# A fused attention and gated-MLP kernel on one core: every second pair of the first chunk's score matmuls in other PSUM banks with VectorE copies, and v's loads three units earlier

## The chip, the cores and the metric

The kernel runs on one core of one Trainium2 chip. The metric is the device time of one execution in microseconds (us). The engines are named as the profile names them: PE (TensorE matmul), PEld (its weight load), DVE (VectorE), ACT (ScalarE), POOL (GpSimd), SP (SyncE), and SPq, POOLq, ACTq for what their queues issue or wait for.

## What is computed

Attention with a mixing of the heads before and after the softmax, and then a bilinear MLP on its output. Sizes: 4 batches, 12 heads, 448 positions, 64 values a head; 768 model columns, 1536 inner ones.

```
scores = scale * q @ k.T                      # per head
scores = einsum("bhij,hg->bgij", scores, w_pre)
attn   = exp(scores - max); attn /= sum + 1e-9
attn   = einsum("bhij,hg->bgij", attn, w_post)
x      = (attn @ v), heads side by side       # 1792 x 768
out    = ((x @ w_a) * (x @ w_b)) @ w_out
```

## The kernel before

**Tiles and order.** The 448 query rows of a batch are cut into chunks of 120, 120, 120 and 88 rows, so there are 16 chunks. For a chunk, `qk` (L219) is called six times. Call i multiplies the q of heads i and i + 6 (two row halves of TensorE) by their keys, into one tile `pst` of two PSUM banks (tag "t", one buffer), and ACT copies both banks at once into `s`, the chunk's scores in SBUF (L227). I call one such call a pair. `s` has two buffers, so chunk c writes where chunk c - 2 lay.

**Units.** A chunk's rows are then taken 20 at a time: a unit, 6 units in a chunk of 120 rows and 5 in the one of 88, 23 in a batch, 92 in all. `gather` (L232) brings a unit's rows of `s` into the order (row, head) on the partitions, with four transfers from SBUF to SBUF on SP's queue (`sb<-s`, L243); unit s + 3 is gathered in iteration s of the main loop (L575), into four buffers. In iteration s, `premix` (L252) multiplies unit s by w_pre into `mp`, `smax` (L265) takes the maximum on DVE and the exponential on ACT, `norm` (L276) works on DVE, and `postmix` (L289) of unit s - 1 multiplies by w_post into `pp`, which ACT copies into `pt` (L307). `av` (L309) multiplies a group of eight units by v into `xp`, two heads' pairs at a time, for the first group of a batch in units 9, 11 and 13, and a DVE copy takes `xp` out (L330).

**What sets the order around the change.** Everything is in program order on each engine, as written. The first chunk's six pairs come ahead of the main loop, one after the other (L558 to L566): its q parts are spread on DVE (`spread_q`, L205), its k parts are loaded on SP (L193), four ahead. Behind them come `setup_w` on DVE (L161), the gathers of units 0 to 3, and `warm_up(WARM3)`: 60 small matmuls into a tile of tag "x" whose result is not used (L136). The tags "m", "p" and "x" have two one-bank buffers each; "m" is next used by the premix, "p" by the postmix, and "x" by that warm-up and by `av`.

The pairs of later chunks are spread over the units. Those of the next batch's first chunk begin in unit 15 of a batch, two of them in that unit, and that chunk's first copy writes the buffer of `s` that the gather of unit 17 reads last. The last chunk of a batch begins in unit 9, and its first copy writes where unit 11 is gathered from.

**Loads.** POOL issues the loads of v, of q from the third chunk on, and of k from the second batch on. The main loop makes it wait once in each iteration for DVE's work of the unit before (`pace`, L118). The six parts of the next batch's v, 224 KB each, are loaded one in an iteration, from unit `V_AT` = 9 of a batch to unit 14 (L595 to L597), k's six parts in units 12 to 16, and q's parts in units 5, 8, 11 and 13 among others. `v` has two buffers for each half of the heads. The first batch's own v is loaded in units 2 and 4. The last batch loads nothing ahead.

After unit 91 the MLP runs from about 475 us to the end, nearly all of it back-to-back matmuls.

Of the kernel before, what the change touches and what calls it, by code (L numbers as in the profile page):

```python
# [7 lines left out]
F32 = mybir.dt.float32  # L8
# [13 lines left out]
def talking_heads_bilinear_kernel(  # L22
# [11 lines left out]
    nc = tc.nc  # L34
    B, _, G, S = k.shape
    H, D = 2 * G, 64
# [5 lines left out]
    QG = 3  # L42
# [18 lines left out]
    WARM3 = 60  # L61
    Q1E = 3
    KL = 3
    V_AT = 9
    LQ = 4
    scale = 1.0 / float(D) ** 0.5

# [1 line left out]
    for b in range(B):  # L69
        t0 = 0  # L70
        while t0 < S:
            n = min(CHUNK, S - t0)
# [23 lines left out]
    ps = ctx.enter_context(tc.tile_pool(name="ps", bufs=2, space=PSUM))  # L96
# [86 lines left out]
    kt, qraw, qt, vt = {}, {}, {}, {}  # L183
    st, sbt, mt, at, ant, ptt, pps, xps = {}, {}, {}, {}, {}, {}, {}, {}

    def load_v(b, i):

        g, e = divmod(i, 3)
        if e == 0:
            vt[b, g] = v_p.tile([P, H // 2, R, D], F32, tag=f"v{g}", name="v")  # L190
        nc.gpsimd.dma_start(out=vt[b, g][:, 2 * e:2 * e + 2], in_=v[b, g][:, 2 * e:2 * e + 2])
# [27 lines left out]
    def qk(c, i):  # L219
        b, t0, n = chunks[c]  # L220
        if c not in st:
            st[c] = big.tile([128, H, S], F32, tag="s", name="s")
        sp = ps.tile([128, 2, 512], F32, tag="t", name="pst", bufs=1)[:, :, :S]
        for g in range(2):
            rows = slice(D * g, D * g + D)
            nc.tensor.matmul(sp[:n, g], lhsT=qt[c, i // QG][rows, i % QG], rhs=kt[b, i][rows])  # L226
        nc.scalar.copy(st[c].rearrange("p (g i) s -> p i g s", g=2)[:n, i], sp[:n])  # L227
# [108 lines left out]
    for c in range(1, NC):  # L336
        b, t0, _ = chunks[c]
        a, e = max(starts[c - 1] - AH, 0), starts[c] - AH
        for i in range(G):
            at_s = qk_at[c, i] = i * Q1E // G if c == 1 else a + i * (e - a) // G  # L340
            items.setdefault(at_s, []).append((qk, c, i))
            if t0 == 0:
                after.setdefault(at_s - KL, []).append((load_k, b, i))
        ready[c] = qk_at[c, G - 1]
        for j in range(G // QG):
            if c > 1:
                when = max(qk_at[c, QG * j] - LQ, 0)
                after.setdefault(when, []).insert(0, (load_q, c, j))
            if c > 1 or j:
                after.setdefault(max(qk_at[c, QG * j] - 1, 0), []).append((spread_q, c, j))  # L350
    last_prep = ready[NC - 1]
    for a in range(NA - 1):
        b, u0, n = groups[a]
# [192 lines left out]
    with tc.manual_schedule():  # L546
# [11 lines left out]
        for i in range(G):  # L558
            if i == 1:
                spread_q(0, 1, nc.vector)  # L560
            if i + 4 < G:
                load_k(0, i + 4)
            if i == 2:
                load_q(1, 0)
                load_q(1, 1)
            qk(0, i)  # L566
# [8 lines left out]
        for s in range(NU + 2):  # L575
# [19 lines left out]
            b, i = divmod(s, NUB)  # L595
            if b + 1 < B and 0 <= i - V_AT < 6:
                load_v(b + 1, i - V_AT)  # L597
            for fn in todo_at.pop(s, ()):
# [89 lines left out]
        for j in range(B * KD):  # L688
            b, m = divmod(j, KD)
# [57 lines left out]
```

## Time and profile before

| what | us |
|---|---|
| median of 3 runs | 1013.9 |
| lowest and highest of the runs | 1010.79, 1014.28 |
| the profiled execution | 1010.31 |
| its span, first to last instruction | 1008.6 |
| PE busy in the span | 962.7 (95%) |
| ACT busy | 418.5 (41%) |
| DVE busy | 513.1 (51%) |
| POOL busy | 293.0 (29%) |

The mean granted TensorE clock over the span is 0.983 of full speed. Start times in the rows below are us from the span's start. In a timeline row stand the start, the duration from first to last instruction of the row, the engine, the line, the operation, its tiles, the count, and in brackets how long the engine had been idle before it and what ended that.

### The profile page before, as it was taken

Reading aid. Unit: us, or ns where it says so; the run is one execution under the profiler, and the core shown is the slowest. Engines: PE = TensorE matmul, PEld = TensorE weight load, DVE = VectorE, ACT = ScalarE, POOL = GpSimd, SP = SyncE. Lnnn points to the kernel's source line nnn. Section 1 sums busy time; section 2 is a strip of 40 time slices with the busy share of each in tenths; the row PEclk is TensorE's granted clock in tenths of the full one; section 3 lists DMA queues with packets and bytes.
Section 4 is the critical chain, followed back from the end, with each engine's and each line's share of the span. In section 5 each row is a group of like instructions: output and inputs, shape, how many; then the busy total and the mean of one; then the engine's idle time right before and its main releaser. Section 6 shows DMA issues by size and latency. Waiting matters only on the chain.

```text
span 1008.6 us, 17007 instructions
## 1 busy us (share of the span) xinstructions
PE 962.7 (95%) x6388; PEld 774.4 (77%) x6388; DVE 513.1 (51%) x1090; ACT 418.5 (41%) x854; POOL 293.0 (29%) x321
## 2 busy tenths in 40 slices
PE   7798899979999899988999999999999999999998
PEld 4465566646665566666889999999999998999997
DVE  1455355535555355567767565665555454432510
ACT  2675466756676566656321111111111133342521
POOL 2223011320123111112133323333233225555542
PEclk9999799989999899999999999999999999999999
DMA  3446233553346333348335333423333256556441
GB/s 117 156 137 199 95 123 123 156 164 97 123 136 191 104 131 119 114 155 260 112 105 188 134 118 138 146 97 139 114 139 136 85 215 244 192 202 257 146 137 68
DMA packets 63472, 146.60 MB, mean 145 GB/s; under 512 B 6252, under 2 KB 48000, under 8 KB 62368
## 3 DMA queue, kind: packets, MB, share of 16 engines
q1 hardware_dynamic: 58528, 131.11, 38.1%
q0 software_dynamic: 4864, 14.42, 5.1%
q8 instruction: 51, 0.84, 0.3%
q14 instruction: 29, 0.24, 0.1%
HBM read 80.23 MB, written 26.74 MB: 106 GB/s over the span
## 4 chain that ended last, share of the span: by engine, by line
PE 82%; DMA 11%; DVE 3%; ACT 2%; SPq 1%; issue 1%; POOL 0%; ACTq 0%; DVEq 0%
PE pp L296 13%; DMA sb<-s 10%; PE pst L226 7%; PE mp L263 7%; PE xp L321 6%; PE po L445 6%; PE po L446 6%; PE po L444 6%; PE pa L444 5%; PE pa L445 5%; PE pa L446 5%; PE pb L446 5%; PE pb L444 5%; PE pb L445 5%; ACT s L227 1%; DVE xhl L376 1%
## 5 line engine op out<-in xcount | busy, mean ns | idle before, releaser
L296 PEld LDWEIGHTS pp<-kr,a 124*112 124x112 f32 (+1 forms) x1440 | 159.7, 182 | 50.7 <-issue 33.0
L272 DVE TENSOR_REDUCE nm<-mp 124x1 f32<-124x448 f32 x180 | 104.2, 619 | 154.3 <-PE mp L263 154.3
L296 PE MATMUL pp<-kr,a 124*112 124x120 f32 (+1 forms) x1440 | 177.3, 278 | 2.8 <-ACT pt L307 1.7
L273 ACT ACTIVATE a<-mp,nm 124x448 f32<-124x448 f32 x180 | 112.7, 631 | 90.7 <-DVE nm L272 90.5
L226 PE MATMUL pst<-k,q 64*120 64x448 f32 (+1 forms) x384 | 100.1, 599 | 30.9 <-ACT s L227 30.8
L406 POOL TENSOR_TENSOR cvm<-cvm,cvr 128x768 int32<-128x768 int32 x36 | 67.0, 1860 | 211.6 <-DVE cvm L405 211.6
L434 POOL TENSOR_TENSOR wl<-rawo,wh 128x768 fp32r<-128x768 f32 x48 | 93.0, 1960 | 100.9 <-ACT wh L433 100.9
L307 ACT COPY pt<-pp 112x480 f32<-112x480 f32 x180 | 97.0, 574 | 51.7 <-PE pp L296 51.6
L456 ACT COPY sa<-pa 128x448 f32<-128x448 f32 x48 | 25.7, 536 | 221.7 <-PE pa L446 216.6
L121 POOL COPY tick<-rs 60x1 f32<-60x1 f32 x92 | 17.1, 186 | 344.9 <-DVE rs L280 344.9
L445 PE MATMUL pa<-xhl,wh 128*128 128x448 f32 x288 | 104.6, 363 | 1.9 <-DVE xhl L376 1.9
L445 PE MATMUL po<-hl,wh 128*128 128x448 f32 x288 | 104.5, 363 | 0.7 <-DVE hl L481 0.7
L444 PE MATMUL pa<-xhl,wh 128*128 128x448 f32 x288 | 104.6, 363 | 0.0
L446 PE MATMUL pa<-xhl,wl 128*128 128x448 f32 x288 | 104.4, 363 | 0.0
L444 PE MATMUL po<-hh,wh 128*128 128x448 f32 x288 | 104.4, 362 | 0.0
L446 PE MATMUL po<-hh,wl 128*128 128x448 f32 x288 | 104.4, 362 | 0.0
L446 PE MATMUL pb<-xhl,wl 128*128 128x448 f32 x282 | 102.3, 363 | 0.9 <-POOL wl L434 0.9
L226 PEld LDWEIGHTS pst<-k,q 64*120 64x120 f32 (+1 forms) x384 | 27.0, 175 | 98.5 <-ACT s L227 39.9
L444 PE MATMUL pb<-xhl,wh 128*128 128x448 f32 x282 | 102.2, 362 | 0.0
L445 PE MATMUL pb<-xhl,wh 128*128 128x448 f32 x282 | 102.2, 362 | 0.0
L227 ACT COPY s<-pst 120x896 f32<-120x896 f32 (+1 forms) x96 | 86.4, 900 | 36.6 <-PE pst L226 19.8
L263 PE MATMUL mp<-sb,wp 60*64 60x448 f32 x720 | 95.2, 564 | 3.8 <-ACT a L273 3.5
(64 smaller groups left out, 1373.1 us busy)
## 6 DMA issues: line engine op xcount, KB each, us to landing
sb<-s SPq DMA_DIRECT2D x356, 105.0 KB
raw<-in_w_ab_dram SPq DMA_DIRECT2D x24, 768.0 KB
rawo<-wod SPq DMA_DIRECT2D x24, 768.0 KB
hd<-hf SPq DMA_DIRECT2D x48, 224.0 KB
raw<-in_w_out_dram SPq DMA_DIRECT2D x12, 768.0 KB
v<-in_v_dram POOLq DMA_DIRECT2D x24, 224.0 KB, 6.0
xhl<-xd SPq DMA_DIRECT2D x12, 448.0 KB
hl<-hd SPq DMA_DIRECT2D x4, 1344.0 KB
```

Of the source, the lines that this page charges most:

```text
L226: nc.tensor.matmul(sp[:n, g], lhsT=qt[c, i // QG][rows, i % QG], rhs=kt[b, i][rows])
L227: nc.scalar.copy(st[c].rearrange("p (g i) s -> p i g s", g=2)[:n, i], sp[:n])
L263: nc.tensor.matmul(mt[u, i // 2][col:col + M], lhsT=wp[r:r + m, :M], rhs=tiles[i % 2][r:r + m])
L272: nc.vector.tensor_reduce(nm[:m], mp[:m], axis=AXX, op=ALU.max, negate=True)
L273: nc.scalar.activation(a[:m], mp[:m], ACTF.Exp, bias=nm[:m], scale=1.0, accum_out=rs[:m])
L296: nc.tensor.matmul(pp[:, r, :, :n], lhsT=an[:m, r * P:(r + 1) * P], rhs=kr[:m, :, :n])
L307: nc.scalar.copy(ptt[a][:P, :, :, o:o + n], pps.pop((u, j))[:, :, :, :n])
L406: lambda: nc.gpsimd.tensor_tensor(m, m, r, op=ALU.add),
L434: nc.gpsimd.tensor_tensor(ll[:, sl], raw, hh.bitcast(F32)[:, sl], op=ALU.subtract)
L444: nc.tensor.matmul(o, lhsT=hh[:, k0 + kk], rhs=mh[:, kk], start=(kk == 0), stop=False)
L445: nc.tensor.matmul(o, lhsT=hh[:, k0 + kk], rhs=ml[:, kk], start=False, stop=False)
L446: nc.tensor.matmul(o, lhsT=ll[:, k0 + kk], rhs=mh[:, kk], start=False, stop=(kk == n - 1))
```

## The change

`qk` treats the first chunk's pairs 1, 3 and 5 in another way. Each of the two heads gets a one-bank tile of its own, of tag "m" for pair 1, "p" for pair 3 and "x" for pair 5, and DVE copies each of the two out by itself. Pairs 0, 2 and 4 stay in `pst` with ACT's copy. Apart from that, `V_AT` goes from 9 to 6, so v's six parts for the next batch are issued in units 6 to 11 of batches 0, 1 and 2.

```diff
-    V_AT = 9
+    V_AT = 6
...
     def qk(c, i):
         b, t0, n = chunks[c]
         if c not in st:
             st[c] = big.tile([128, H, S], F32, tag="s", name="s")
+        if c == 0 and i % 2:
+            for g in range(2):
+                rows = slice(D * g, D * g + D)
+                sp = ps.tile([128, 512], F32, tag="mpx"[i // 2], name="psq")[:, :S]
+                nc.tensor.matmul(sp[:n], lhsT=qt[c, i // QG][rows, i % QG], rhs=kt[b, i][rows])
+                nc.vector.tensor_copy(st[c][:n, g * G + i], sp[:n])
+            return
         sp = ps.tile([128, 2, 512], F32, tag="t", name="pst", bufs=1)[:, :, :S]
```

## Rows read from the trace of the kernel before

**Rows 1.** The page's part 4: the chain of work that ended last, by engine and by line, in shares of the whole span.
```profile
PE 82%; DMA 11%; DVE 3%; ACT 2%; SPq 1%; issue 1%; POOL 0%; ACTq 0%; DVEq 0%
PE pp L296 13%; DMA sb<-s 10%; PE pst L226 7%; PE mp L263 7%; PE xp L321 6%; PE po L445 6%; PE po L446 6%; PE po L444 6%; PE pa L444 5%; PE pa L445 5%; PE pa L446 5%; PE pb L446 5%; PE pb L444 5%; PE pb L445 5%; ACT s L227 1%; DVE xhl L376 1%
```

**Rows 2.** The timeline of all engines from 0 to 45 us: the first chunk's pairs, the warm-up behind them, the first gather and the first premix.
```profile
5.51 1.03 PE L226 MATMUL pst<-k,q 64*120 64x448 f32 x4
...
6.10 0.79 DVE L211 COPY q<-qraw 128x360 f32<-128x360 f32 x1 [2.00 <-DMA qraw<-in_q_dram]
6.59 0.91 ACT L227 COPY s<-pst 120x896 f32<-120x896 f32 x1 [4.28 <-PE pst L226]
...
7.55 1.02 PE L226 MATMUL pst<-k,q 64*120 64x448 f32 x4 [1.01 <-ACT s L227]
...
9.68 0.81 POOL L211 COPY q<-qraw 128x360 f32<-128x360 f32 x1 [4.61 <-DMA qraw<-in_q_dram]
...
15.63 1.71 PE L226 MATMUL pst<-k,q 64*120 64x448 f32 x4 [1.00 <-ACT s L227]
...
17.28 4.44 PE L141 MATMUL warm<-ones 128*128 128x128 f16 x60
...
18.32 27.11 SPq L243 DMA_DIRECT2D sb<-s  x28
...
22.94 1.79 PE L263 MATMUL mp<-sb,wp 60*64 60x448 f32 x6 [0.33 <-DMA sb<-s]
```

**Rows 3.** The transfers' rate from 0 to 22 us, in 40 slices of 0.55 us each.
```profile
GB/s 0 0 0 92 264 348 295 257 211 344 282 244 287 376 393 379 81 16 0 0 0 134 196 5 0 0 0 0 0 0 0 0 0 0 30 0 121 124 127 127
```

**Rows 4.** All DVE copies of line 330, which take a PSUM bank out as the new copies do: durations in ns, least, median and most, and their shapes.
```profile
L330 DVE COPY xs<-xp x24: 557/656/658, 78.8 to 488.8; 128x480 f32<-128x480 f32 x16, 128x384 f32<-128x384 f32 x8
```

**Rows 5.** Stretches of the start: from and to, length, then busy us (and count) of PE, PEld, DVE, ACT and POOL, the granted clock, the DMA share and GB/s.
```profile
6.00:15.50 9.50, 4.61 (x20) 1.15 (x16) 1.77 (x6) 4.45 (x5) 2.19 (x3) 1.00 0.38 124
...
16.00:19.00 3.00, 3.00 (x21) 1.73 (x18) 0.00 (x0) 0.91 (x1) 0.00 (x0) 0.50 0.03 5
...
33.00:36.00 3.00, 3.00 (x15) 3.00 (x16) 0.00 (x0) 1.47 (x2) 1.27 (x2) 0.50 0.93 248
```

**Rows 6.** PE's timeline: the postmixes of units 0 and 1.
```profile
32.92 3.53 PE L296 MATMUL pp<-kr,a 124*112 124x120 f32 x16
...
41.26 1.89 PE L296 MATMUL pp<-kr,a 124*112 124x120 f32 x16
```

**Rows 7.** The chain that ended last, in order of time: start, us, what. These are its pieces on the gather's transfers in batch 0 (four of them) and in batch 1 (two).
```profile
47.94 8.21 DMA sb<-s
...
56.16 7.02 DMA sb<-s
...
63.20 8.59 DMA sb<-s
...
94.44 10.00 DMA sb<-s
...
195.30 10.05 DMA sb<-s
...
205.36 10.81 DMA sb<-s
```

**Rows 8.** Transfers issued between 56.16 and 63.20 us, other than the gather's: count, KB each, median us from issue to landing.
```profile
qraw<-in_q_dram POOLq DMA_DIRECT2D x1, 132.0 KB, 5.5
```

**Rows 9.** The same between 63.20 and 71.80 us.
```profile
v<-in_v_dram POOLq DMA_DIRECT2D x2, 224.0 KB, 6.0
```

**Rows 10.** The same between 195.30 and 205.34 us, with the gather's.
```profile
sb<-s SPq DMA_DIRECT2D x7, 105.0 KB
k<-in_k_dram POOLq DMA_DIRECT2D x3, 224.0 KB, 7.5
v<-in_v_dram POOLq DMA_DIRECT2D x2, 224.0 KB, 6.4
xd<-xs SPq DMA_DIRECT2D x1, 240.0 KB
qraw<-in_q_dram POOLq DMA_DIRECT2D x1, 180.0 KB, 6.6
```

**Rows 11.** ACT's timeline: the first copy of a batch's last chunk (unit 9 of batch 0 and of batch 1) and of the next batch's first chunk (unit 15 of batches 0, 1 and 2).
```profile
71.94 0.90 ACT L227 COPY s<-pst 88x896 f32<-88x896 f32 x1 [3.62 <-DMA sb<-s]
...
104.67 0.91 ACT L227 COPY s<-pst 120x896 f32<-120x896 f32 x1 [6.59 <-DMA sb<-s]
...
185.22 0.89 ACT L227 COPY s<-pst 88x896 f32<-88x896 f32 x1
...
217.54 0.91 ACT L227 COPY s<-pst 120x896 f32<-120x896 f32 x1 [3.29 <-DMA sb<-s]
...
330.28 0.91 ACT L227 COPY s<-pst 120x896 f32<-120x896 f32 x1 [3.27 <-DMA sb<-s]
```

**Rows 12.** PE's timeline: the pair of unit 10 in batch 0 and in batch 1, and the second pair of unit 15 in batch 1 with the postmix behind it.
```profile
72.90 0.99 PE L226 MATMUL pst<-k,q 64*88 64x448 f32 x4 [0.76 <-ACT s L227]
...
189.07 0.99 PE L226 MATMUL pst<-k,q 64*88 64x448 f32 x4
...
218.50 1.85 PE L226 MATMUL pst<-k,q 64*120 64x448 f32 x4 [5.49 <-ACT s L227]
220.28 3.54 PE L296 MATMUL pp<-kr,a 124*112 124x120 f32 x16
```

## The prediction

> **What bounds the kernel now.** I read the shares of the chain that ended last first. It runs mainly on PE, and the only other large share is the gather's transfers with 10% [rows 1]. PE's own share in the units is not touched by the change, so the questions are the start, where PE waits, and the pieces on `sb<-s`.
>
> At the start the timeline shows one step repeated six times: a pair of matmuls takes 1.02 us, ACT's copy 0.91 us, and the next pair waits for that copy because `pst` has one buffer [rows 2]. Pairs start at 5.51 and 7.55, so a step is about 2.02 us. PE stands idle half of it. In the stretch from 6 to 15.5 it is busy for 4.61 of 9.5 us, and after that the granted clock goes to 0.50, that is 1.2 GHz [rows 5]; the sixth pair takes 1.71 us [rows 2]. The gather starts at 18.32, when ACT's last copy is out, and the premix waits for its rows at 22.94, 4.62 us after the first issue [rows 2].
>
> Later the pieces on `sb<-s` matter. In batch 0 they follow each other from 47.94 to 94.44 + 10.00 = 104.44 with hardly a gap; in batch 1 they begin at 195.30 [rows 7]. Each ends at ACT's first copy into a chunk buffer whose rows were still being gathered: 6.59 us of ACT's waiting at 104.67, 3.29 at 217.54 and 3.27 at 330.28 [rows 11]. In batch 1 PE then stood idle for 5.49 us, and its next work ran at half the clock: a pair in 1.85 us and a postmix in 3.54 [rows 12], where 1.02 [rows 2] and 1.89 [rows 6] are usual.
>
> **The pairs in other banks.** Removed are three of ACT's copies, 0.91 us each. Added are six DVE copies of one bank, 448 columns. DVE's nearest are its copies of line 330, 557 ns for 384 columns and 656 to 658 for 480 [rows 4]; between them, 448 columns give 0.62 us, 1.25 for a pair. The trace shows no DVE copy of this very shape, so 0.56 and 0.66 are the bounds.
>
> Pairs 1, 3 and 5 no longer need `pst`, so each runs in the gap that PE has now while ACT copies the pair before it. Pair 0 runs 5.5 to 6.6, pair 1 to 7.6, pair 2 to 8.6, and so on; two pairs take one step of 2.02 us, and the sixth ends near 5.5 + 3 x 2.02 = 11.6. Its two DVE copies end at 12.4 if the first starts with the first half's result, at 12.9 if both wait for the whole pair. I take 12.7. The gather then starts 18.32 - 12.7 = 5.6 us earlier (5.4 to 5.9).
>
> What must hold for that:
> - The operands are there. The second q part lands at 6.10 and is spread by 6.89 [rows 2]; pair 3 needs it at 8.6. By the rate [rows 3] the bytes up to k's third part (1.06 MB in the order of issue) are moved by 6.0 us and up to the fourth (1.29 MB) by 6.6; the second q part lands about 1.1 us after its bytes, so these land near 7.1 and 7.7 and are wanted at 7.6 and 8.6. The sixth was issued ahead of chunk 1's q, which POOL finds landed at 9.68 [rows 2], and is wanted at 10.6. The margin of the third part, half a microsecond, is the least. If it is missing, the step slips by as much.
> - DVE keeps up: 1.25 us of copies in each 2.02 us. `setup_w` now comes behind them; DVE is busy for 1.77 us in 6 to 15.5 [rows 5], of which 0.79 is the spread, so it takes about 1 us and ends by 14, and the premix, which needs `wp`, comes at 12.7 + 4.62 = 17.3.
> - The warm-up behind the pairs now waits for DVE to free a buffer of tag "x", until 12.3 at most. With its present 4.44 us [rows 2] it ends by 16.8, still ahead of the premix's rows. Nothing else is queued behind it on PE but that premix.
>
> At the start the row decides the clock: it fell after PE was busy for about half of a stretch [rows 5], and the new stretch is full from 5.5 to 11.6. So I take 1.02 us for the sixth pair and not 1.71. The Trainium skill (TensorE: Matmul & The Clock Gate, Part 1: The HAM clock gate) says that the throttled state is the default and that activity releases it; by that the sixth pair is fast too, whereas at 1.71 us the shift of the gather would be 0.7 us smaller. The trace agrees as far as it goes.
>
> From there on everything is started by its place in the program, v's first loads too, so the 5.6 us should stay. One thing can move: the slow spell around 33 to 36 [rows 5], which costs 3.53 - 1.89 = 1.6 us in one postmix [rows 6], may vanish (-1.6) or fall elsewhere. I count it as 0.
>
> **v's loads.** In each of batches 0, 1 and 2 three of six loads leave units 12 to 14 and three come into units 6 to 8; units 9 to 11 have one as before. What is a load worth to a gather behind it? From 56.16 to 63.20 the piece of 7.02 us [rows 7] has one small q load beside it [rows 8], that of 8.59 us has two v loads [rows 9]: 1.57 / 2 = 0.79 each. The piece of 10.05 us holds seven gathers and seven other transfers [rows 10]; with 7.02 / 8 = 0.88 a gather, that leaves (10.05 - 6.14) / 7 = 0.56. I take 0.65, in the middle, so three loads are worth 1.95 us (1.7 to 2.4).
>
> - Batches 1 and 2: the loads of units 12 to 14 are issued within the pieces that end at ACT's wait. It shrinks from 3.29 and 3.27 [rows 11] to about 1.3: a gain of 2 x 1.95 = 3.9. The slow spell behind it costs (1.85 - 1.02) + (3.54 - 1.89) = 2.5 us each time. PE's idle time would be 5.49 - 1.95 = 3.5 us; idle times of 1.01 left the clock, 5.49 lost it, and 3.5 is nearer to the latter. I leave the spells in.
> - Batch 0: the pieces are unbroken since 47.94, so all six loads are within them before and after. The end at 104.44 stays: 0. At unit 9 ACT waits for 3.62 us already and PE for 0.76 at unit 10 [rows 11, 12]; that grows to some 2.7 and is taken from the wait at unit 15. Bounds: -1.95 if the transfers do have gaps, +1.95 if it isn't given back.
> - What the three loads meet in units 6 to 8: in batch 1 ACT's copy of unit 9 comes at 185.22 without a wait [rows 11]. Even if its rows had landed just then, 1.95 us more would let it end at 185.22 + 1.95 + 0.89 = 188.1, and PE wants the bank at 189.07 [rows 12]. Hidden by `av` and a postmix; without that cover it would cost 1.95. On POOL each issue takes under 1 us ahead of a q load and a spread that PE needs an iteration later: 0.
>
> **Sum.** -5.6 - 3.9 = -9.5 on the profiled 1010.31, or 1000.8. The median of the runs lies 3.6 us (0.36%) above that execution, so it becomes 1004.4.
>
> **Rivals.**
> - *The clock stays.* With 3.5 us of idle time instead of 5.5 PE keeps 2.4 GHz at unit 15 of batches 1 and 2: a further 2 x 2.5 us, 999.4. For it: the 1.01 us gaps kept it. Against it: half-busy stretches lost it at the start [rows 5]. The skill's same page (HAM oscillation) says that the clock is lost when a wait is long enough; no row lies between.
> - *The loads don't matter.* The gather's queue finds its gaps again, or batch 0 loses at unit 9 what the others gain. Then only the start counts: 1013.9 - 5.6 = 1008.3, close to the limit of what can be told.
> - *The start doesn't shift.* The odd pairs' copies or missing k parts hold PE as ACT's copies do. Then 1013.9 - 3.9 = 1010.0: no change that can be told.
> - *Slower.* The gather's queue is full in units 6 to 8, and the three loads push unit 11's rows so late that PE waits at unit 10 for over 3 us and loses the clock there in all three batches, while unit 15 stays as it is. Each would cost about 1.95 + 2.5, or 13.4 in all, less 5.6: 1021.7. It decides from 189.07 - 0.89 = 188.2 on as the landing of those rows in batch 1. Against it: no wait there now, and almost 3 us of room.
>
> **How the numbers follow.** Forecast 0.50 (1001.5 to 1007), clock stays 0.22, loads don't matter 0.17, start doesn't shift 0.06, slower 0.05. About 0.5%, 5 us, is what a measurement of this kernel can tell from no change, that is 1008.8. The forecast, the clock's case and a third of the third give faster 0.78; the rest of that and the fourth 0.17 the same; 0.05 slower. The range reaches from 998, most of the clock's case, to 1010, the fourth; the costs' bounds (0.3 at the start, 0.9 at the loads, 1.95 in batch 0) lie inside.
>
> **What the profile after would show.** Right: PE without gaps from 5.5 to about 11.6, the first gather issued near 12.7, the premix's wait ending near 17.3, chunk starts 5.6 us earlier up to unit 9; ACT's waits at unit 15 of batches 1 and 2 near 1.3 us. Wrong: gaps between the first pairs, the first gather after 14; waits at unit 15 of 3 us still, or new ones at unit 9 of batches 1 and 2 that PE feels.

## The result, and the profile after

The changed kernel takes 994.5 us (median; 993.35 to 995.44) against 1013.1 beside it: a ratio over the runs of 0.9829, with a 95% interval of 0.9803 to 0.9855 (the two medians alone give 0.9816, inside it). So it is faster, by 1.5 to 2.0% or some 18 us, where 9.5 us were forecast; the time lies below the range of 998 to 1010. The profiled execution took 994.56 us with a span of 992.7, 15.9 less than the span before.

Where the time went is read by laying the same event of both traces side by side. POOL's `tick` copy stands once in every unit, when DVE has come to the unit's `norm`. These are POOL's rows of units 8, 11 and 16 of batch 0, unit 16 of batches 1 and 2, and the last unit, first before the change:

```profile
64.34 0.18 POOL L121 COPY tick<-rs 60x1 f32<-60x1 f32 x1 [1.65 <-DVE rs L280]
...
79.67 0.18 POOL L121 COPY tick<-rs 60x1 f32<-60x1 f32 x1 [2.66 <-DVE rs L280]
...
113.98 0.18 POOL L121 COPY tick<-rs 60x1 f32<-60x1 f32 x1 [13.85 <-DVE rs L280]
...
226.74 0.18 POOL L121 COPY tick<-rs 60x1 f32<-60x1 f32 x1 [10.43 <-DVE rs L280]
...
339.43 0.18 POOL L121 COPY tick<-rs 60x1 f32<-60x1 f32 x1 [10.37 <-DVE rs L280]
...
474.62 0.18 POOL L121 COPY tick<-rs 60x1 f32<-60x1 f32 x1 [4.06 <-DVE rs L280]
```

and after it:

```profile
58.96 0.18 POOL L121 COPY tick<-rs 60x1 f32<-60x1 f32 x1 [1.15 <-DVE rs L287]
...
79.26 0.18 POOL L121 COPY tick<-rs 60x1 f32<-60x1 f32 x1 [4.29 <-DVE rs L287]
...
105.72 0.18 POOL L121 COPY tick<-rs 60x1 f32<-60x1 f32 x1 [6.00 <-DVE rs L287]
...
214.21 0.18 POOL L121 COPY tick<-rs 60x1 f32<-60x1 f32 x1 [6.16 <-DVE rs L287]
...
322.79 0.18 POOL L121 COPY tick<-rs 60x1 f32<-60x1 f32 x1 [6.25 <-DVE rs L287]
...
458.77 0.18 POOL L121 COPY tick<-rs 60x1 f32<-60x1 f32 x1 [4.06 <-DVE rs L287]
```

The differences are -5.38, -0.41, -8.26, -12.53, -16.64 and -15.85 us. Between the steps that follow they don't change by more than 0.1 until the last batch. So the saving comes in four steps: 5.38 at the start; a loss of 4.97 between the ticks of units 9 and 11 of batch 0; a gain of 7.85 at unit 15 of batch 0; and gains of 4.27 and 4.11 at unit 15 of batches 1 and 2. About 0.8 is lost again around the entry to the MLP.

**The start.** The timeline of all engines after the change, to be read against [rows 2]:

```profile
5.51 1.36 PE L233 MATMUL pst<-k,q 64*120 64x448 f32 x4
...
6.71 0.92 PE L227 MATMUL psq<-k,q 64*120 64x448 f32 x4
...
7.66 1.16 DVE L228 COPY s<-psq 120x448 f32<-120x448 f32 x2 [0.74 <-PE psq L227]
7.88 1.02 PE L233 MATMUL pst<-k,q 64*120 64x448 f32 x4 [0.26 <-ACT s L234]
...
10.75 0.92 PE L227 MATMUL psq<-k,q 64*120 64x448 f32 x4
...
11.70 1.16 DVE L228 COPY s<-psq 120x448 f32<-120x448 f32 x2 [0.86 <-PE psq L227]
12.38 3.51 PE L141 MATMUL warm<-ones 128*128 128x128 f16 x60 [0.71 <-DVE s L228]
...
12.92 32.82 SPq L250 DMA_DIRECT2D sb<-s  x35
...
17.56 1.79 PE L270 MATMUL mp<-sb,wp 60*64 60x448 f32 x6 [0.72 <-DMA sb<-s]
```

Each odd pair lies in what was PE's gap. The gather starts at 12.92 in place of 18.32, and the premix follows 4.64 us later as before. The last pair takes 0.92 us in place of 1.71, and the warm-up 3.51 in place of 4.44: the clock wasn't lost there (it is granted in full from 5.5 to 11.6).

**ACT's waits**, to be read against [rows 11]: ACT's timeline at unit 9 of batch 0, and at unit 15 of batches 0, 1 and 2.

```profile
69.90 0.90 ACT L234 COPY s<-pst 88x896 f32<-88x896 f32 x1 [6.96 <-DMA sb<-s]
...
97.56 0.90 ACT L234 COPY s<-pst 120x896 f32<-120x896 f32 x1
...
205.99 0.91 ACT L234 COPY s<-pst 120x896 f32<-120x896 f32 x1
...
314.57 0.91 ACT L234 COPY s<-pst 120x896 f32<-120x896 f32 x1
```

At unit 9 the wait has grown from 3.62 to 6.96. At unit 15 the waits of 6.59, 3.29 and 3.27 are gone altogether. PE's rows show what that is worth. Before the change, besides [rows 12], the second pair of unit 15 stood so in batch 0, with the postmix behind it, and in batch 2:

```profile
105.62 1.85 PE L226 MATMUL pst<-k,q 64*120 64x448 f32 x4 [8.78 <-ACT s L227]
107.40 3.54 PE L296 MATMUL pp<-kr,a 124*112 124x120 f32 x16
...
331.24 1.85 PE L226 MATMUL pst<-k,q 64*120 64x448 f32 x4 [5.47 <-ACT s L227]
```

After it, the pair of unit 10 in batch 0, and the second pair of unit 15 in batches 0, 1 and 2, each with the postmix behind it:

```profile
70.85 1.60 PE L233 MATMUL pst<-k,q 64*88 64x448 f32 x4 [3.71 <-ACT s L234]
72.38 2.92 PE L303 MATMUL pp<-kr,a 124*112 124x120 f32 x16
...
98.51 1.85 PE L233 MATMUL pst<-k,q 64*120 64x448 f32 x4 [2.09 <-ACT s L234]
100.29 2.62 PE L303 MATMUL pp<-kr,a 124*112 124x120 f32 x16
...
206.95 1.22 PE L233 MATMUL pst<-k,q 64*120 64x448 f32 x4 [2.19 <-ACT s L234]
208.09 3.31 PE L303 MATMUL pp<-kr,a 124*112 124x120 f32 x16
...
315.53 1.02 PE L233 MATMUL pst<-k,q 64*120 64x448 f32 x4 [2.28 <-ACT s L234]
316.48 3.21 PE L303 MATMUL pp<-kr,a 124*112 124x120 f32 x16
```

In batch 1 PE's idle time falls from 5.49 to 2.19 (-3.30); the pair and the postmix behind it, at the lower clock still for a part of the time, fall by 0.63 and 0.23; with the premix's 0.1 that is the 4.27 of the ticks. What is left, about 2.1 us in all three batches, is not a wait for transfers: unit 15 has two pairs and one `pst`. In batch 0 PE's idle time at unit 15 falls from 8.78 to 2.09, but PE now idles for 3.71 us at unit 10 and loses the clock there too.

### The profile page after: what moved, and what is told of

Its sections match the earlier page's. It is cut to its first block, busy times and chain, and to the rows that moved or that the text cites. A ratio compares the mean times of both kernels' runs of the same rounds, so it can differ in the third digit from the quotient of the medians.

```text
span 992.7 us, 17003 instructions
## 1 busy us (share of the span) xinstructions
PE 960.2 (97%) x6388; PEld 772.8 (78%) x6388; DVE 518.8 (52%) x1096; ACT 416.0 (42%) x851; POOL 292.6 (29%) x321
## 3 DMA queue, kind: packets, MB, share of 16 engines
q0 software_dynamic: 4864, 14.42, 5.0%
## 4 chain that ended last, share of the span: by engine, by line
PE 89%; DMA 4%; DVE 3%; ACT 2%; SPq 1%; issue 1%; POOL 0%; ACTq 0%; DVEq 0%
PE pp L303 16%; PE mp L270 8%; PE pst L233 8%; PE xp L328 7%; PE po L452 6%; PE po L453 6%; PE po L451 6%; PE pa L451 5%; PE pa L453 5%; PE pa L452 5%; PE pb L453 5%; PE pb L452 5%; PE pb L451 5%; DMA sb<-s 1%; DMA xhl<-xd 1%; DVE xhl L383 1%
## 5 line engine op out<-in xcount | busy, mean ns | idle before, releaser
L233 PE MATMUL pst<-k,q 64*120 64x448 f32 (+1 forms) x372 | 96.6, 596 | 16.1 <-ACT s L234 16.0
L488 DVE TENSOR_TENSOR hl<-hl,hh 128x448 fp32r<-128x448 f32 x48 | 57.4, 1252 | 75.9 <-ACT hh L487 75.9
L473 DVE TENSOR_TENSOR hf<-pb,sa 128x448 f32<-128x448 f32 x47 | 29.3, 624 | 124.2 <-PE pb L453 121.7
```

## The experiments

Two theories stood at first. **A:** a load of 224 KB delays the gather behind it by more than the 0.65 us of the prediction. **B:** it is worth 0.65, and the rest came from where the earlier start puts the units against clock and transfers. The kernel before took 1011.3, 1010.1 and 1011.1 us beside the three groups of experiments, so their times are best compared by the ratios.

**The banks alone** (`e1_banks_only`):

```diff
-    V_AT = 6
+    V_AT = 9
```

> The pairs in other banks alone; v's loads stay in units 9 to 14. Both theories: the first gather at 12.9, all units 5.4 us earlier, the waits at unit 15 of 6.6, 3.3 and 3.3 us as before; 1013.1 - 5.4 = 1007.7. If the clock's spells fall elsewhere, up to 2 us either way.

Measured: 1003.04 us, ratio 0.9919 (0.9890 to 0.9949). The first gather starts at 12.86, and unit 0 ends 5.46 us earlier. A further 1.6 comes by unit 2: there is no slow spell in the first 90 us, and unit 0's postmix takes 1.89 and not 3.53. The waits stay, in ACT's timeline at units 9 and 15 of batch 0, and 15 of batches 1 and 2:

```profile
67.35 0.90 ACT L234 COPY s<-pst 88x896 f32<-88x896 f32 x1 [5.95 <-DMA sb<-s]
...
98.31 0.91 ACT L234 COPY s<-pst 120x896 f32<-120x896 f32 x1 [4.82 <-DMA sb<-s]
...
211.83 0.91 ACT L234 COPY s<-pst 120x896 f32<-120x896 f32 x1 [4.20 <-DMA sb<-s]
...
323.11 0.91 ACT L234 COPY s<-pst 120x896 f32<-120x896 f32 x1 [2.39 <-DMA sb<-s]
```

So the start is worth its 5.4 us, by itself, and that spell goes or stays from one profiled execution to the next (it stayed in the changed kernel's, near 27 us). The time lies 4.7 us below the 1007.7 expected, outside the 2 us allowed: 1.6 are that spell, some 2 that the kernel before took 1011.3 and not 1013.1 beside it, and the rest is open.

**The loads alone** (`e2_v_only`): the kernel before, with

```diff
-    V_AT = 9
+    V_AT = 6
```

> v's loads alone in units 6 to 11; the first chunk as before. Theory A (a load of 224 KB delays the gather behind it by about 1.1 us, wherever the start lies): as in the changed kernel, ACT's wait at unit 15 gone in batches 0 to 2, that at unit 9 of batch 0 grown from 3.6 to 7.0; 1013.1 - 10.4 = 1002.7. Theory B (a load is worth 0.65 us, as predicted; what went beyond came from where the earlier start puts the units against the clock and the transfers): waits of about 1.3 us stay at unit 15, and the time is about 1009 to 1010.

Measured: 1000.6 us, ratio 0.9890 (0.9854 to 0.9926), 10.7 us less than before. In this execution the start was 1.2 us late and lost the clock. Waits at unit 15: 2.42 us in batch 0, none in batch 1, 0.51 in batch 2; 5.70 at unit 9 of batch 0. The expected time was 1002.7 by A and 1009 to 1010 by B, and the ticks give 4.38 and 3.69 us in batches 1 and 2. So the loads by themselves bring more than twice the 3.9 that were forecast there, without the earlier start, and B falls. Batch 0 is another matter: from unit 7 to unit 16 this execution wins only 0.3 us (the premixes of units 8 and 9 wait for their rows, and 2.3 us are lost there), and that of the banks alone loses 0.3, where the changed kernel's wins 2.9. The two parts, 8.3 and 10.7 us, add up to about the whole within their intervals.

**One and two loads moved** (`e3_v8`, `e4_v7`): the changed kernel with

```diff
-    V_AT = 6
+    V_AT = 8   # and 7
```

> As the changed kernel, but v's loads in units 8 to 13: one load leaves the stretch ahead of unit 15 and one comes ahead of unit 9. Theory A: wait at unit 15 of batches 1 and 2 about 3.3 - 1.1 = 2.2 us, at unit 9 of batch 0 3.6 + 1.1 = 4.7. Theory B: 2.65 and 4.3. Time between 1000 and 1006.

> As the changed kernel, but v's loads in units 7 to 12: two loads moved. Theory A: wait at unit 15 of batches 1 and 2 about 1.1 us, at unit 9 of batch 0 5.8. Theory B: 2.0 and 4.9. Time between 996 and 1003.

Measured: 1000.63 us, ratio 0.9895 (0.9860 to 0.9929), and 994.97 us, ratio 0.9839 (0.9808 to 0.9871). ACT's timeline at unit 15 of batches 1 and 2, with the loads from unit 8 on:

```profile
209.76 0.91 ACT L234 COPY s<-pst 120x896 f32<-120x896 f32 x1 [2.50 <-DMA sb<-s]
...
322.26 0.91 ACT L234 COPY s<-pst 120x896 f32<-120x896 f32 x1 [2.82 <-DMA sb<-s]
```

and from unit 7 on:

```profile
205.91 0.91 ACT L234 COPY s<-pst 120x896 f32<-120x896 f32 x1 [0.82 <-DMA sb<-s]
...
314.94 0.91 ACT L234 COPY s<-pst 120x896 f32<-120x896 f32 x1 [0.52 <-DMA sb<-s]
```

Means of the two batches: 3.29 with the loads from unit 9 (the kernel before and the banks alone, four waits from 2.39 to 4.20), 2.66 from unit 8, 0.67 from unit 7, none from unit 6. Two loads take away 2.62 us, or 1.3 each, unevenly: the first alone takes 0.63, which is B's price, and with waits that differ by up to 1.8 us under the same loads it doesn't decide by itself. From unit 7 on the wait is all but gone, and the time is that of the changed kernel: the third load moved buys nothing that can be told. At unit 9 of batch 0 ACT waits for 6.69 and 5.80 us, where A had 4.7 and 5.8; the time with two loads moved lies just below its range.

That place gives a second measure: when ACT's copy starts there, counted from the first gather's issue, for it starts when unit 11's rows have landed. It is 53.6 us (kernel before), 54.5 (banks alone) and 53.7 (`e11_v_on_sp`, below) with the loads from unit 9, 55.6 and 55.8 from units 8 and 7, 56.8 to 57.7 in the five kernels with loads from unit 6, and 52.6 to 52.9 in `e6_no_v`, `e7_v16` and `e8_best`, which load later or not at all. (In `e6_no_v` and `e11_v_on_sp` the trace names a PE instruction as what ended the wait; by the program the copy needs only its pair, which was long done, and the gathered rows.) From unit 9 to unit 6 that is 3.1 us in the mean for three loads, 1.0 each, again unevenly. Theory A holds in the mean of several loads, with 1.0 to 1.3 us a load.

**No loads ahead** (`e6_no_v`):

```diff
-                load_v(b + 1, i - V_AT)
+                if i == V_AT:
+                    vt[b + 1, 0], vt[b + 1, 1] = vt[0, 0], vt[0, 1]
```

> As the changed kernel, but leaves out the loads of v for batches 1 to 3 (these batches use batch 0's v), so only q and k are loaded ahead. Theory A (1.1 to 1.3 us a load): ACT's wait at unit 9 of batch 0 falls from 7.0 to 3.0 - 3.7, PE's idle time there from 3.7 to about 1 and the clock stays; no wait at unit 15; 994.5 - 4 = 990.5. Theory B (0.65): wait at unit 9 about 5, 994.5 - 2 = 992.5. Both: nothing in batches 1 and 2.

Measured: 991.68 us (987.3 to 992.04), ratio 0.9821 (0.9798 to 0.9843). At unit 9 of batch 0 ACT starts its copy at 66.66 after 3.97 us of waiting, 52.6 us after the first gather's issue and 4.4 earlier by that measure than with loads in units 6 to 9; PE idles for 1.10 us. The wait is near A's 3.0 to 3.7 and not B's 5. The time doesn't decide: the median lies between the two forecasts, and the profiled execution, at 987.3, below both. In that execution 1.7 us come from a place where neither expected anything, unit 15 of batch 1, where the clock stayed (see below).

**Loads on the gather's own queue** (`e11_v_on_sp`): why does a load cost that much? Either its bytes occupy the transfer engines that the gather uses, or two queues take turns.

```diff
-    V_AT = 6
+    V_AT = 9
...
-        nc.gpsimd.dma_start(out=vt[b, g][:, 2 * e:2 * e + 2], in_=v[b, g][:, 2 * e:2 * e + 2])
+        (nc.sync if b else nc.gpsimd).dma_start(out=vt[b, g][:, 2 * e:2 * e + 2], in_=v[b, g][:, 2 * e:2 * e + 2])
```

> The other banks, and v's loads in units 9 to 14 as before the change, but for batches 1 to 3 issued on SP's queue, where the gather's transfers go, and not on POOL's. Theory A1 (a load's price is the time that its bytes take on the transfer engines that the gather uses): waits at unit 15 as with the loads on POOL's queue, 2.4 to 4.8 us, 1003. Theory A2 (the price comes from two queues taking turns): in one queue a load costs about 0.6 us, waits near 1.5 us at unit 15, 997.

Measured: 1002.21 us, ratio 0.9921 (0.9902 to 0.9940): as the banks alone. ACT at unit 15 of batches 0, 1 and 2:

```profile
98.05 0.91 ACT L234 COPY s<-pst 120x896 f32<-120x896 f32 x1 [5.08 <-DMA v<-in_v_dram]
...
209.29 0.91 ACT L234 COPY s<-pst 120x896 f32<-120x896 f32 x1 [2.42 <-DMA v<-in_v_dram]
...
321.09 0.91 ACT L234 COPY s<-pst 120x896 f32<-120x896 f32 x1 [2.35 <-DMA sb<-s]
```

In batches 0 and 2 the waits are those of the other queue (4.82 and 2.39), in batch 1 2.42 stands against 4.20; none is near A2's 1.5. So the price doesn't need two queues taking turns. (In one queue a gather also stands behind a whole load; that this costs the same by another way is not excluded.) That it is the engines' time fits, and the page of before gives an estimate: POOL's queue moved 14.42 MB in 5.1% of the engines' time over 1008.6 us, which is 51.4 x 0.229 / 14.42 = 0.82 us of every engine for a load. What a load costs beyond that, 0.2 to 0.5 us, stays open.

**What is left at unit 15** was tried in two ways. First, PE's idle time filled with the warm-up's matmuls (`e5_warm_gap`):

```diff
-            for it in items.get(s, ()):
+            for n_, it in enumerate(items.get(s, ())):
+                if s > 3 and n_ and it[0] is qk and items[s][n_ - 1][0] is qk:
+                    warm_up(36)
                 it[0](*it[1:])
```

> As the changed kernel, with 36 of the warm-up's matmuls (2.0 us at full clock) put into PE's idle 2.2 us between unit 15's two pairs. Theory: the slow spell that still follows there comes from that idle time and costs about 1.5 us in each of three batches; full clock through unit 16, 994.5 - 4.5 = 990. Rival: the spell comes from something else, nothing changes, or the added matmuls delay the second pair: 994 to 996.

PE's timeline at unit 15 of batch 1:

```profile
203.55 2.18 PE L141 MATMUL warm<-ones 128*128 128x128 f16 x36
205.71 1.02 PE L233 MATMUL pst<-k,q 64*120 64x448 f32 x4
206.65 1.89 PE L303 MATMUL pp<-kr,a 124*112 124x120 f32 x16
```

The pair and the postmix are at full clock (1.02 and 1.89 in place of 1.22 and 3.31), and by the ticks the three places give 1.60, 1.73 and 1.65 us. So the spell came with the idle time: filled, the clock stays in three of three places. The Trainium skill (TensorE: Matmul & The Clock Gate, HAM oscillation) ties losing the clock to PE's idle gaps; the trace agrees in so far as work that computes nothing keeps it. But an idle time of this length doesn't always cost the clock. In `e7_v16` (below) the same place of batch 1 kept it, granted 1.00 from 200 to 206 us, as it did in `e6_no_v` after 2.09 us:

```profile
201.24 1.02 PE L233 MATMUL pst<-k,q 64*120 64x448 f32 x4 [2.08 <-ACT s L234]
202.19 1.89 PE L303 MATMUL pp<-kr,a 124*112 124x120 f32 x16
```

Both lost it in batches 0 and 2, after 2.08 to 2.14 us. What decides between them is open. The time of `e5_warm_gap` itself, 991.69 us, ratio 0.9825 (0.9801 to 0.9850), doesn't show the gain: the profiled execution lost 5.5 us again in its last part (see the end), and whether the others did is not known.

Second, the two pairs moved to unit 19 (`e9_late_double`):

```diff
-            at_s = qk_at[c, i] = i * Q1E // G if c == 1 else a + i * (e - a) // G
+            at_s = qk_at[c, i] = i * Q1E // G if c == 1 else a + (i * (e - a) + 4) // G
```

> As the changed kernel, but the unit with two pairs of the next batch's first chunk is unit 19 (which has v's matmuls) and not 15. Theory: what is left at unit 15, 2.2 us of PE's idle time and a slow spell of about 1.5 us in three batches, comes from the two pairs in one unit and goes: 994.5 - 10 = 984.5. Rival: it moves to unit 19: 994.5.

Measured: 992.72 us (989.78 to 997.82), ratio 0.9835 (0.9799 to 0.9871). The rival holds: unit 19's second pair in batch 1 starts after 2.08 us of idle time, and `av` behind it runs slow (3.90 us in place of 2.39). Unit 15 is 4.7 us better, and unit 19 gives that back, because v's matmuls stand behind both pairs.

With v's matmuls between the two pairs (`e10_between`: the edit above, and)

```diff
+    for s_, its in items.items():
+        pair = [it for it in its if it[0] is qk]
+        if len(pair) == 2 and len(its) > 2:
+            its.remove(pair[1])
+            its.append(pair[1])
```

> As the changed kernel (v's loads in units 6 to 11), with the two pairs in unit 19 and v's matmuls between them. Theory: as the changed kernel without what is left at unit 15, 994.5 - 9 = 985. Rival: the earlier copy at unit 15 meets the gather again (a wait of 0.8 us was seen) or the idle time stays at unit 19: 992 or more.

Measured: 983.47 us, ratio 0.9740 (0.9719 to 0.9761), near the forecast 985. No idle time over 1.2 us is left at units 15 and 19, and no slow spell but those near 28 and 73 us and at the MLP's entry. At unit 9 of batch 0 ACT waits for 6.79.

**The loads behind both waiting places** (`e7_v16`):

```diff
-    V_AT = 6
+    V_AT = 16
```

> As the changed kernel, but v's loads in units 16 to 21, behind both waiting places. Theory A: as without the loads, 990.5, if the gather has room there. Rival: the wait moves to unit 20, where the second chunk of the next batch begins (ACT waits there 1.3 us a load, 2 to 4 us, in three batches): 995 to 1000.

Measured: 986.34 us, ratio 0.9770 (0.9749 to 0.9791), better than expected; at unit 9 of batch 0 the wait is 4.22 and the clock stays. Units 16 to 21 have room, and no wait arises at unit 20. By the ticks this execution is 8.3 us ahead of the changed kernel's: 4.4 at units 9 and 10 of batch 0, 1.7 because the clock stayed at unit 15 of batch 1, 1.3 because the spell near 27 us is missing, and 0.8 at the entry to the MLP. The second and third of these go or stay between executions, so the loads' place itself is worth less than the whole. **With both** (`e8_best`: `V_AT = 16`, and the edits of `e10_between`):

> v's loads in units 16 to 21, the unit with two pairs is unit 19, and there v's matmuls (2.3 us on PE) come between the two pairs. Theory: the copy that the second pair waits for is hidden by them, so the 2.1 us of idle time and the spell of 1.6 us behind it go in three batches; on the 986.3 of the loads alone: 986.3 - 6 to - 11, 975 to 980. Rival: the loads in units 16 to 19 hold up the gather that unit 20's copy waits for, and the gain is lost there: 984 to 988.

Measured: 978.98 us, ratio 0.9688 (0.9673 to 0.9703). This beats the changed kernel by 1.4%. PE's timeline at unit 19 of batch 1 shows the second pair directly behind `av`, without a wait:

```profile
211.58 2.39 PE L328 MATMUL xp<-pt,v 112*64 112x160 f32 x32
213.90 1.02 PE L233 MATMUL pst<-k,q 64*120 64x448 f32 x4
214.85 1.89 PE L303 MATMUL pp<-kr,a 124*112 124x120 f32 x16
```

**The first batch's own v earlier** (`e12_first_v`), on top of that:

```diff
         spread_q(1, 0)
+        for i in range(3):
+            load_v(0, i)
         setup_w()
...
-            if s in (2, 4):
+            if s == 2:
                 for i in range(3):
-                    load_v(0, 3 * (s // 2 - 1) + i)
+                    load_v(0, 3 + i)
```

> As e8_best, with the first batch's own v loaded earlier: three parts ahead of the main loop, when the transfer engines are free, and three in unit 2. Theory A: fewer loads among the first gathers, ACT's wait at unit 9 of batch 0 falls from 4.2 by 1 to 3 us, PE's idle time of 1.4 there goes: 1 to 2 us less than e8_best. Rival: the first gathers are delayed by the three parts by as much as is won: no change.

Measured: 980.67 us (978.92 to 984.44), ratio 0.9712 (0.9686 to 0.9738): no gain. The wait at unit 9 is gone, as expected, but the rival came with it. PE's row of the first premix:

```profile
20.00 1.95 PE L270 MATMUL mp<-sb,wp 60*64 60x448 f32 x6 [0.73 <-DMA sb<-s]
```

Its rows come 6.86 us after the first gather's issue, at 13.14, where it was 4.63 in `e8_best`: the three parts hold the first gather up by 2.2 us. Behind that wait the clock fell to 0.54 between 21 and 26 us, and unit 1's tick comes 5.1 us later than in `e8_best`. That the wait brought the loss of the clock is not shown by a run of its own.

## Why the prediction was wrong

- **The start was right.** Forecast 5.6 us (5.4 to 5.9), measured 5.38 by the ticks, 5.40 by the gather's issue. Pairs fill the gaps, DVE's two copies take 1.16 us (1.25), the gather starts at 12.92 (12.7), and the premix's wait ends at 17.56 (17.3). The operands were there, with `setup_w` and the warm-up hidden. The sixth pair kept the clock.
- **The failing step is the price of a load**, "I take 0.65, in the middle, so three loads are worth 1.95 us (1.7 to 2.4)". The mechanism is right, the size is not: in the mean of several loads it measures 1.0 to 1.3 each. The term for batches 1 and 2 was 3.9 and measured 8.4: ACT's waits went from 3.29 and 3.27 to nothing and not to 1.3, PE's idle time fell by 3.30 and 3.19, to the 2.2 that the two pairs leave, and the rest is clock.
- **Why the division gave too little** is shown in part. I divided by the loads *issued* within a piece, but a load lands some 6 us after its issue [rows 9]. What POOL's queue moved in the pieces of 7.02, 8.59 and 10.05 us (packets, MB, share of the engines) is this:

```profile
q0 software_dynamic: 21, 0.08, 4.8%
...
q0 software_dynamic: 162, 0.44, 17.8%
...
q0 software_dynamic: 402, 1.29, 44.5%
```

The piece of 7.02 us was nearly free of loads, as I took it to be. That of 8.59 us holds 0.36 MB more, 1.6 loads and not two, so 1.57 us are 1.0 a load and not 0.79. The lower end isn't mended in this way: 1.29 MB are 5.6 loads, and (10.05 - 6.14) / 5.6 is still only 0.70. Why that piece gives less than the moved loads cost stays open.
- **Batch 0: 0 was forecast, 2.9 came.** At unit 10 PE's idle time grew to 3.71 (2.7 forecast) and the clock went, a loss of 4.97. Taken back was more than the loss: 7.85 at unit 15. "The end at 104.44 stays" failed: shifted by the start it would be 99.1, and ACT copied at 97.56 without a wait. The second pair there starts 7.11 us earlier, 1.73 more than the start's 5.38, which the bound for gaps among the transfers (1.95) allows; the other 1.15 is a clock that came back sooner, the postmix in 2.62 in place of 3.54 and the premix in 0.98 in place of 1.21. Neither part of the change wins this alone (0.3 us lost with the banks, 0.3 won with the loads); why the two together do is not shown.
- **The rival "the clock stays"** did not come true, though its 999.4 is the nearest of the times. The clock fell at unit 15 in all three batches after idle times of 2.09 to 2.28 us, shorter than the 3.5 of that rival, but for a shorter time: a pair and a postmix cost 1.6 us over the usual in batch 1 where they cost 2.5. That the spell comes with the idle time was shown by the warm-up's matmuls in the gap. "No row lies between" held for the rows shown, and not for the trace of before: there an idle time of 1.93 us stands ahead of the slow postmix of unit 0 [rows 6], and one of 2.01 us ahead of unit 1's, which kept its 1.89. Idle times of about 2 us can go either way here, in other runs as well.
- **Not seen:** that with the wait gone 2.1 us of PE's idle time are left in each batch, from two pairs in one unit. I put ACT's whole wait down to the transfers, which was right; that 5.49 us of PE's idle time less 3.29 of ACT's wait leave 2.2 with another cause, the prediction doesn't say.
- The rivals "the loads don't matter", "the start doesn't shift" and "slower" fall: either part alone is faster, and no wait came up at unit 9 of batches 1 and 2.

## What to carry to other kernels

Bulk loads belong behind the place where an engine waits for a small transfer's last bytes: here one that fell in the same stretch cost 1.0 to 1.3 us in the mean, more than the 0.8 us of engine time estimated for its bytes, and moving all six behind both such places won 6 us more by the ratios than moving them by three units. To price a load from a trace, count the bytes that moved in a stretch and not the issues, and don't rely on it: here even that gave 0.7 to 1.0. Moving some and looking at the wait gave the price. When a wait goes, ask what the engine behind it waits for next: here a second pair on one buffer, cured by putting other matmuls between.

## What the runs showed of the hardware

The last part, 24 blocks of 36 matmuls, ran at two speeds at a granted clock of 1.00: 7.20 us a block in the changed kernel, 7.44 in the profiled executions of `e5_warm_gap` and `e9_late_double`, with the same instructions (5.5 us in all). The other twelve profiled executions show 533.5 to 534.2 us from the last unit's tick to the end, these two 539.5. The cause is open. It can hide gains of this size, which the ticks of the units still show.
